# Windowed attention followed by a maxout feed-forward layer: the order of work between chunk 1 and chunk 5 rewritten, and V of chunk 2 requested later

## The chip, the cores and the metric

The kernel runs on one core of a Trainium2 chip. The metric is the device time of one execution in microseconds (us). Work on the core is done by TensorE (PE for matmuls, PEld for the loading of the stationary operand), VectorE (DVE), ScalarE (ACT) and GpSimd (POOL). SyncE (SP) issues most DMAs. Each engine takes its instructions in the order in which the program lists them.

## The reference, cut to what matters

Inputs are q, k and v of 4 batches, 8 heads, 768 positions and 64 dimensions, three weights of 512 x 768 and an output weight of 768 x 512. Each query sees the 4 first positions ("sinks") and the last 128.

```python
scores = scale * np.matmul(q, k.transpose(0, 1, 3, 2))
keep = is_sink | in_window            # rel = i - j; 0 <= rel < 128
scores = np.where(keep, scores, -1e9)
a = softmax(scores)                   # over the keys
x = concat_heads(np.matmul(a, v))     # 3072 x 512
h = np.maximum(np.maximum(x @ w1, x @ w2), x @ w3)
out = h @ w_out                       # 3072 x 512, float32
```

## The kernel before, in words

The 3072 tokens are cut into 12 chunks (`ci`) of 256, three to a batch. A chunk passes through these helpers, each of which emits its instructions on the spot:

- `load` requests q, k or v of a chunk on SP's queue, 512 KB each. Each kind has two buffers, so chunk 3's q goes where chunk 1's was. A `gate` is a one-element write by POOL into the buffer ahead of the load: the load has to wait for it, and so it sets when the load may be issued. `after(wi, c)` copies an element of weight `wi`, column `c`, so POOL first waits until that piece of the weight has landed; `pool_gate` is a plain memset.
- `load_w` and `load_wo` request weights on POOL's own DMA queue: three pieces of 256 columns for each of the three weights (`w1`, `w2`, `w3` of the reference are `w_sb[0]`, `[1]`, `[2]`), two for the output weight.
- `cast_qk` and `cast_v` turn the loaded float32 into bf16 on the engine named in the call; `turn` transposes q or k on PE and copies the result out of PSUM; `turn_dma` does it by a DMA on SP (chunk 4 on).
- `score` (PE), `expo` (ACT) and `mask` (DVE) make the masked exponentials of a pair of heads (`p` = 0 to 3). `sink_score` and `av_open` add the sinks; `av` multiplies with V on PE into a PSUM bank, and then divides by the row sum on DVE (a reciprocal, L476, and a multiplication, L479).
- `xpose` transposes x on PE and copies it out; `xpose_dma` does it by DMA (chunk 3 on).
- `ffn_h(ci, fp, wi)` multiplies a third (`fp`) of the hidden columns with weight `wi`, 8 matmuls, and takes the result from PSUM: for `wi` 0 a copy (ACT as a rule), for 1 and 2 a running maximum on DVE (L527). `ffn_y(ci, t)` is the output product of half a chunk, 6 matmuls.

There are eight PSUM banks. `bank` gives out the one that came free longest ago, in the order of the program, and the matmul that writes it waits for its last reader.

What is run when is an order written out by hand: the calls for chunks 0 to 5 stand one after another (L626 to L877), and a loop with a fixed pattern follows for the chunks after that. While chunk 0 and 1 are still in attention, the weights arrive; the feed-forward work of chunks 0 and 1 is held back and put between the attention work of chunks 1 and 2.

Of the kernel before, what the change touches and what calls it, by code (L numbers as in the profile page):

```python
# [16 lines left out]
def kernel(  # L17
# [13 lines left out]
    nc = tc.nc  # L31
# [12 lines left out]
    DS = d_model // 128  # L44
# [4 lines left out]
    with tc.manual_schedule():  # L49
# [239 lines left out]
        def load_w(wi, c0=0, c1=None):  # L289
            c1 = d_ff if c1 is None else c1  # L290
            w = (moe_w1, moe_w2, moe_w3)[wi]
            nc.gpsimd.dma_start(out=w_sb[wi][:, :, c0:c1],  # L292
                                in_=w.rearrange("(a p) f -> p a f", p=128)[:, :, c0:c1])
# [98 lines left out]
        def expo(ci, p):  # L392
            if ci >= NEW:
                return expo4(ci, p)
            lo = 0 if ci % CPB else 1
            e, st = es[ci, p]
            for a in range(2):
                nc.scalar.activation(e[:, a, lo:], st[a][:, lo:], AF.Exp, scale=scale)  # L398
                give(st[a])
# [43 lines left out]
        os_ = {}  # L443
# [13 lines left out]

        xs = {}

        def av(ci, p):  # L460
            b, c = divmod(ci, CPB)
            o = os_[ci, p]
            e = es[ci, p][0]
            first = c == 0
            for t in range(2):
                for a in range(2):
                    blocks = [(1, ci, 0)] if t == 0 else [(2, ci, 0), (3, ci, 1)]
                    if t == 0 and c:
                        blocks = [(0, ci - 1, 1)] + blocks
                    for s, cv, n in blocks:  # L470
                        nc.tensor.matmul(  # L471
                            o[:, t, a], lhsT=e[:, a, s], rhs=vb[cv % RING][:, n, 2 * p + a],
                            start=first, stop=True, skip_group_check=True)
                        first = False
            rc = work.tile([128, 2, 2], F32, tag="rc", bufs=4, name="rc")
            nc.vector.reciprocal(rc, o[:, :, :, D])  # L476
            if ci not in xs:
                xs[ci] = work.tile([128, NP, 2, 2, D], BF16, tag="x", bufs=2, name="x_sb")
            nc.vector.tensor_mul(xs[ci][:, p], o[:, :, :, 0:D],  # L479
                                 rc.unsqueeze(3).to_broadcast([128, 2, 2, D]))  # L480
            give(o)

        xTs = {}

        def xpose(ci, t, eng=None):
            eng = eng or nc.scalar
            if t == 0:
                xTs[ci] = work.tile([128, DS, 2, 128], BF16, tag="xT", bufs=3, name="xT")
            pt = bank([128, DS, 128], BF16, "xt")
            for ds in range(DS):  # L490
                nc.tensor.transpose(
                    pt[:, ds], xs[ci][:, ds, t].rearrange("q a d -> q (a d)"), ident)
            (nc.scalar.copy if eng is nc.scalar else eng.tensor_copy)(xTs[ci][:, :, t], pt)
            give(pt)
# [6 lines left out]

        hs = {}

        def ffn_h(ci, fp, wi, cuts=1, eng=nc.scalar):
            if ci not in hs:
                hs[ci] = work.tile([128, FB, 256], BF16, tag="h", bufs=3, name="h_sb")
            hp = bank([128, 2, 256], F32, "h_ps")
            for f in range(2):
                c0 = (2 * fp + f) * 128
                for ds in range(DS):  # L510
                    x = xTs[ci][:, ds]
                    if ci < NEW:
# [4 lines left out]
                    nc.tensor.matmul(  # L517
                        hp[:, f].rearrange("q (i t r) -> q i t r", i=2, r=x.shape[3]),
                        lhsT=w_sb[wi][:, ds, c0:c0 + 128], rhs=x,
                        start=(ds == 0), stop=(ds == DS - 1))  # L520
            dst = hs[ci][:, 2 * fp:2 * fp + 2]
            if wi == 0:
                (nc.scalar.copy if eng is nc.scalar else eng.tensor_copy)(dst, hp)  # L523
            else:
                for f in range(cuts):
                    x = slice(2 * f // cuts, 2 * (f + 1) // cuts)
                    nc.vector.tensor_max(dst[:, x], dst[:, x], hp[:, x])  # L527
            give(hp)
# [170 lines left out]
        sink_v(0)  # L699
        expo(1, 3)  # L700
        ffn_h(0, 2, 0, 1, nc.vector)
        score(1, (2,))
        load(2, 'q', part=1, parts=2)
        load(2, 'q', part=0, parts=2, gate=pool_gate)
        load_w(2, 0, 256)
        expo(1, 2)
        load_w(2, 256, 512)
        load_w(2, 512, 768)
        mask(1, 3)
        ffn_h(0, 1, 0)  # L710
        mask(1, 2)
        av_open(1)
        ffn_h(0, 0, 0)
        av(1, 0)
        load(2, 'v', gate=after(0, 300))
        av(1, 3)
        av(1, 1)
        av(1, 2)
        ffn_h(0, 2, 1)
        ffn_h(0, 1, 1)  # L720
        xpose(1, 0, nc.vector)
        xpose(1, 1, nc.scalar)
        ffn_h(0, 0, 1)
        cast_qk(2, 'k', 1, nc.gpsimd)
        ffn_h(1, 2, 0)
        cast_qk(2, 'k', 0, nc.scalar)
        ffn_h(1, 0, 0)
        ffn_h(1, 1, 0)
        load_wo()
        load(3, 'q', gate=after(2, 300))  # L730
        load(3, 'k')
        factors(msk0[0], addm0)
        turn(2, 'k', 0, nc.vector)
        ffn_h(1, 0, 1)
        cast_v(2, 1, 0, nc.gpsimd)
        turn(2, 'k', 1, nc.scalar)
        ffn_h(1, 1, 1)
        cast_qk(2, 'q', 1, nc.scalar)
        cast_qk(2, 'q', 0, nc.vector)
        ffn_h(1, 2, 1)  # L740
        ffn_h(1, 1, 2)
        turn(2, 'q', 1, nc.scalar)
        ffn_h(0, 0, 2)
        turn(2, 'q', 0, nc.scalar)
        ffn_h(0, 1, 2)
        score(2, (0,))
        expo(2, 0)
        score(2, (3,))
        score(2, (1,))
        cast_v(2, 1, 1, nc.gpsimd)  # L750
        sink_score(2)
        expo(2, 1)
        mask(2, 0)
        load(3, 'v', gate=after(1))
        cast_v(2, 0, 0, nc.gpsimd)
        expo(2, 3)
        ffn_h(1, 0, 2)
        cast_v(2, 0, 1, nc.gpsimd)
        ffn_h(0, 2, 2)
        ffn_h(1, 2, 2)  # L760
        score(2, (2,))
        load(4, 'q', gate=after(0, 300))
        cast_qk(3, 'q', 0, nc.gpsimd)
        av_open(2)
        load(4, 'k', gate=after(0))
        mask(2, 1)
        expo(2, 2)
        cast_qk(3, 'k', 0, nc.gpsimd)
        load(4, 'v')
        mask(2, 3)  # L770
        mask(2, 2)
        cast_qk(3, 'q', 1, nc.vector)
        ffn_y(0, 0)
        ffn_y(0, 1)
        av(2, 0)
        turn(3, 'q', 0, nc.scalar)
        cast_qk(3, 'k', 1, nc.scalar)
        load(5, 'q')
        av(2, 2)
        load(5, 'k', gate=after(0, 300))  # L780
        av(2, 3)
        turn(3, 'q', 1, nc.scalar)
        av(2, 1)
        ffn_y(1, 0)
        turn(3, 'k', 1, nc.scalar)
        turn(3, 'k', 0, nc.scalar)
        xpose(2, 0, nc.scalar)
        xpose(2, 1, nc.vector)
        ffn_y(1, 1)
        cast_qk(4, 'q', 1, nc.vector)  # L790
        cast_v(3, 0, 0, nc.gpsimd)
        cast_v(3, 0, 1, nc.gpsimd)
        score(3, (1,))
        cast_v(3, 1, 1, nc.gpsimd)
        cast_qk(4, 'q', 0, nc.vector)
        expo(3, 1)
        score(3, (0,))
        cast_qk(4, 'k', 0, nc.vector)
        cast_qk(4, 'k', 1, nc.gpsimd)
        mask(3, 1)  # L800
        ffn_h(2, 0, 0)
        cast_v(4, 1, 0, nc.gpsimd)
        cast_v(3, 1, 0, nc.vector)
        score(3, (3,))
        turn_dma(4, 'k')
        turn_dma(4, 'q')
        expo(3, 0)
        expo(3, 3)
# [172 lines left out]
```

## Time and profile before

| | us |
|---|---|
| median of 3 runs (lowest to highest) | 176.03 (175.41 to 176.61) |
| the profiled execution, whole | 175.3 |
| its span in the profile | 173.6 |
| TensorE busy | 167.1 |
| VectorE / GpSimd / ScalarE busy | 124.7 / 110.9 / 88.7 |

The profile is of one execution; the difference of 1.7 us between its time and its span lies around the program. The granted TensorE clock was full (1.0) throughout. The 16 DMA engines were at nine tenths or more in nearly every slice of the first 48 us, since inputs and weights come in at the same time there. Times in the profile's views count from the span's start; L numbers are lines of the kernel before.

### The profile page before, as it was taken

The numbers are of one execution on the slowest core, as the hardware profiler recorded it, in microseconds if no ns is written. First come the engines' busy times: TensorE is split into PE (matmuls) and PEld (weight loads), VectorE is DVE, ScalarE is ACT, GpSimd is POOL, SyncE is SP. The second block draws the span as 40 slices with busy tenths as digits, with TensorE's granted clock in tenths as the row PEclk, the third lists the DMA queues.
The fourth block names the chain that finished last, engine by engine and source line by source line (L and its number), as shares of the span: only waits on it lengthen the run. The fifth ranks groups of instructions, "written<-read, shape, count | busy, mean of one in ns | idle before, by whom it ended". The sixth has DMA issues, their size and how long they took to land.

```text
span 173.6 us, 5416 instructions
## 1 busy us (share of the span) xinstructions
PE 167.1 (96%) x2225; PEld 128.6 (74%) x2225; DVE 124.7 (72%) x262; ACT 88.7 (51%) x183; POOL 110.9 (64%) x193
## 2 busy tenths in 40 slices
PE   7979999999999999999999999999999999999992
PEld 2546888857696697797797797797797896896871
DVE  3387854796797985986877976877777776776361
ACT  4778544677954614817726717717636516510210
POOL 7399507545499999999999999999998600000000
PEclk9999999999999999999999999999999999999999
DMA  4999999999999997988999999989999119017303
GB/s 139 301 288 198 218 217 256 221 306 276 280 195 216 190 273 124 245 199 216 253 199 252 195 224 246 265 168 227 264 195 259 32 33 377 21 34 272 121 2 121
DMA packets 71545, 35.22 MB, mean 203 GB/s; under 512 B 27488, under 2 KB 69984, under 8 KB 71520
## 3 DMA queue, kind: packets, MB, share of 16 engines
q1 hardware_dynamic: 65824, 31.60, 79.0%
q0 software_dynamic: 5552, 3.15, 12.7%
q8 instruction: 17, 0.28, 0.7%
q10 hardware_dynamic: 144, 0.13, 0.2%
q14 instruction: 8, 0.07, 0.1%
HBM read 25.17 MB, written 6.29 MB: 181 GB/s over the span
## 4 chain that ended last, share of the span: by engine, by line
PE 85%; DMA 7%; POOL 5%; issue 1%; DVE 0%; POOLq 0%; SPq 0%
PE h_ps L517 52%; PE y_ps L564 11%; PE y_ps L540 7%; PE o L471 6%; DMA w<-in_moe_w_dram 4%; PE st L357 3%; DMA v_raw<-in_v_dram 3%; PE st L331 2%; POOL w L292 2%; POOL vb L123 1%; PE pt L138 1%; PE o L453 1%; PE y_ps L586 1%; PE sk L423 1%; POOL q_bf L118 0%
## 5 line engine op out<-in xcount | busy, mean ns | idle before, releaser
L517 PE MATMUL h_ps<-xT,w 128*128 128x256 bf16 x864 | 101.2, 273 | 0.2 <-DMA w<-in_moe_w_dram 0.2
L517 PEld LDWEIGHTS <-w 128*128 128x128 bf16 x864 | 81.7, 98 | 10.7 <-issue 0.5
L527 DVE TENSOR_TENSOR h_sb<-h_sb,h_ps 128x512 bf16<-128x512 bf16 (+1 forms) x74 | 49.0, 670 | 17.4 <-PE h_ps L517 15.6
L523 ACT CAST h_sb<-h_ps 128x512 bf16<-128x512 f32 x35 | 20.6, 589 | 51.3 <-PE h_ps L517 51.2
L129 POOL CAST vb<-v_raw 32x512 bf16<-32x512 f32 x48 | 36.8, 766 | 2.5 <-DMA v_raw<-in_v_dram 0.3
L90 POOL CAST k_bf<-k_raw 32x512 bf16<-32x512 f32 x48 | 29.6, 616 | 2.2
L398 ACT ACTIVATE e_sb<-st 128x512 bf16<-128x512 f32 (+1 forms) x48 | 23.1, 583 | 1.1 <-PE st L331 1.1
L479 DVE TENSOR_TENSOR x_sb<-o,rc 128x256 bf16<-128x256 f32 x48 | 20.4, 424 | 1.7
L564 PE MATMUL y_ps<-wo,h_sb 64*64 64x512 bf16 (+1 forms) x312 | 21.1, 377 | 0.0
L471 PE MATMUL o<-vb,e_sb 128*128 128x65 bf16 x352 | 16.5, 193 | 0.8 <-DVE vb L123 0.8
L471 PEld LDWEIGHTS <-e_sb 128*128 128x128 bf16 x352 | 14.5, 97 | 3.1 <-ACT e_sb L398 1.0
L123 POOL CAST vb<-v_raw 64x512 bf16<-64x512 f32 x18 | 12.6, 697 | 5.7 <-DMA v_raw<-in_v_dram 5.1
L389 DVE TENSOR_TENSOR e_sb<-e_part,msk 128x1024 bf16<-128x1024 bf16 x16 | 13.1, 831 | 3.3 <-ACT e_part L374 3.1
L406 DVE TENSOR_TENSOR e_sb<-e_sb,msk 128x1024 bf16<-128x1024 bf16 (+1 forms) x18 | 13.6, 776 | 2.3 <-ACT e_sb L398 2.1
L564 PEld LDWEIGHTS <-h_sb 64*64 64x64 bf16 (+1 forms) x312 | 9.9, 106 | 5.0
L374 ACT ACTIVATE e_part<-st 128x384 bf16<-128x384 f32 x32 | 13.1, 495 | 0.5 <-PE st L357 0.5
L540 PE MATMUL y_ps<-wo,h_sb 128*128 128x512 bf16 x54 | 12.8, 380 | 0.0
L476 DVE RECIPROCAL rc<-o 128x4 f32<-128x4 f32 x48 | 8.4, 174 | 4.0 <-PE o L471 3.8
L118 POOL CAST k_bf<-k_raw 128x512 bf16<-128x512 f32 x6 | 3.8, 650 | 9.5 <-PE pt L138 6.8
L118 ACT CAST q_bf<-q_raw 128x512 bf16<-128x512 f32 x13 | 7.6, 620 | 3.0 <-DMA q_raw<-in_q_dram 3.0
L540 PEld LDWEIGHTS <-h_sb 128*128 128x128 bf16 x54 | 4.8, 98 | 5.4 <-DVE h_sb L527 0.8
L427 ACT ACTIVATE e_sink<-sk 128x256 bf16<-128x256 f32 x8 | 3.1, 389 | 10.0 <-PE sk L423 10.0
(90 smaller groups left out, 142.9 us busy)
## 6 DMA issues: line engine op xcount, KB each, us to landing
k_raw<-in_k_dram SPq DMA_DIRECT2D x11, 512.0 KB, 5.6
v_raw<-in_v_dram SPq DMA_DIRECT2D x11, 512.0 KB, 5.6
q_raw<-in_q_dram SPq DMA_DIRECT2D x10, 512.0 KB, 6.9
out_dram<-y_sb SPq DMA_DIRECT2D x9, 512.0 KB, 3.1
w<-in_moe_w_dram POOLq DMA_DIRECT2D x9, 256.0 KB, 6.1
q_raw<-in_q_dram SPq DMA_DIRECT2D x4, 256.0 KB, 7.6
out_dram<-y_sb SPq DMA_DIRECT2D x1, 1024.0 KB, 5.3
wo<-in_moe_w_out_dram POOLq DMA_DIRECT2D x2, 384.0 KB, 8.0
```

The costliest lines, as they stand in the source:

```text
L90: f(bfs[ci, "k"][x:x + 32, :, n], raws[ci, "k"][y:y + 32, :, i].rearrange("q (p a) d -> q p a d", a=2))
L123: eng.tensor_copy(vb[ci % RING][64 * i:64 * i + 64, n, :, 0:D], raws[ci, "v"][64 * n:64 * n + 64, :, i])
L129: eng.tensor_copy(vb[ci % RING][x:x + 32, n, :, 0:D], raws[ci, "v"][y:y + 32, :, i])
L398: nc.scalar.activation(e[:, a, lo:], st[a][:, lo:], AF.Exp, scale=scale)
L406: (eng or nc.vector).tensor_mul(e[:, :, lo:], e[:, :, lo:], msk0[0] if lo else msk)
L471: nc.tensor.matmul(o[:, t, a], lhsT=e[:, a, s], rhs=vb[cv % RING][:, n, 2 * p + a], start=first, stop=True, skip_group_check=True)
L479: nc.vector.tensor_mul(xs[ci][:, p], o[:, :, :, 0:D], rc.unsqueeze(3).to_broadcast([128, 2, 2, D]))
L517: nc.tensor.matmul(hp[:, f].rearrange("q (i t r) -> q i t r", i=2, r=x.shape[3]), lhsT=w_sb[wi][:, ds, c0:c0 + 128], rhs=x, start=(ds == 0 ...
L523: (nc.scalar.copy if eng is nc.scalar else eng.tensor_copy)(dst, hp)
L527: nc.vector.tensor_max(dst[:, x], dst[:, x], hp[:, x])
L540: nc.tensor.matmul(yp, lhsT=hs[ci][:, fb, t * 128:(t + 1) * 128], rhs=wo[:, fb], start=(fb == 0), stop=(fb == FB - 1))
L564: nc.tensor.matmul(yps[ci][t][c:c + cols], lhsT=hs[ci][hp, fb, x:x + cols], rhs=wo[hp, fb], start=(turn == 0 and fb == 0), stop=(turn == 1 ...
```

## The change

The calls from the last scores of chunk 1 to the first casts of chunk 5 stand in another order. So that they can be put more finely, four helpers get a switch: `av(..., then=False)` leaves the division to a later call of `norm`, `ffn_h(..., then=False)` leaves the maximum to a later `ffn_max`, and `xpose` takes the order in which the four pairs are transposed.

```diff
-        def av(ci, p):
+        def av(ci, p, then=True):
...
+            if then:
+                norm(ci, p)
+
+        def norm(ci, p):
+            o = os_[ci, p]
             rc = work.tile([128, 2, 2], F32, tag="rc", bufs=4, name="rc")
             nc.vector.reciprocal(rc, o[:, :, :, D])
...
-        def xpose(ci, t, eng=None):
+        def xpose(ci, t, eng=None, order=range(DS)):
...
-            for ds in range(DS):
+            for ds in order:
...
+            maxima[ci, fp, wi] = hp
+            if then:
+                ffn_max(ci, fp, wi, cuts, eng)
+
+        def ffn_max(ci, fp, wi, cuts=1, eng=nc.scalar):
+            hp = maxima.pop((ci, fp, wi))
...
-        load(2, 'v', gate=after(0, 300))
...
+        load(2, 'v', gate=after(2, 600))
...
-        cast_v(2, 1, 1, nc.gpsimd)
...
+        cast_v(2, 1, 1, nc.vector)
...
-        cast_v(2, 0, 1, nc.gpsimd)
...
+        cast_v(2, 0, 1, nc.vector)
```

No instruction is added or taken away, and each stays on its engine, but for the two casts of V of chunk 2 that go from POOL to DVE.

The last scores of chunk 1 (pair 2) now come after `av_open(1)` and `av(1, 1)`; `ffn_h(0, 1, 1)` comes after the transposes of chunk 1 rather than ahead of them; `ffn_h(1, 2, 0)` and `(1, 1, 0)` come ahead of `ffn_h(0, 0, 1)`, the first user of the last piece of weight 1. Three `ffn_y` halves come ahead of `av_open(2)` where there were two. The transposes of chunk 3 come ahead of `ffn_y(1, 1)` and those of x of chunk 2 after it; three scores of chunk 3 come ahead of `ffn_h(2, 0, 0)` rather than two.

The first place is on VectorE, at chunk 1: `e_sb` is what `mask` works on, `rc` and `x_sb` are the division after `av`, `h_sb` a maximum or copy of the feed-forward. Before:

```order
L523 CAST h_sb<-h_ps 128x512
L406 TENSOR_TENSOR e_sb<-e_sb,msk 128x1024 x2
L476 RECIPROCAL rc<-o 128x4
L479 TENSOR_TENSOR x_sb<-o,rc 128x256
L476 RECIPROCAL rc<-o 128x4
L479 TENSOR_TENSOR x_sb<-o,rc 128x256
```

After, with the numbers of the new lines:

```order
L536 CAST h_sb<-h_ps 128x512
L406 TENSOR_TENSOR e_sb<-e_sb,msk 128x1024
L481 RECIPROCAL rc<-o 128x4
L484 TENSOR_TENSOR x_sb<-o,rc 128x256
L406 TENSOR_TENSOR e_sb<-e_sb,msk 128x1024
L481 RECIPROCAL rc<-o 128x4
L484 TENSOR_TENSOR x_sb<-o,rc 128x256
```

The first division (pair 1, which needs no mask) moves between the two masks; three divisions follow as before.

The second place is on GpSimd, where gates, weight requests and casts share one queue: `w_109` is weight 2, `w_107` weight 0, `v_raw` and `q_raw` the buffers that a gate writes to, `vb_79` V of chunk 2 in bf16. Before:

```order
L602 CAST k_raw<-w_107 1x1
L606 MEMSET q_raw 1x1
L292 DMA w_109<-in_moe_w_dram 128x4x256 x3
L602 CAST v_raw<-w_107 1x1
L118 CAST k_bf<-k_raw 128x2x2x2x64
L300 DMA wo<-in_moe_w_out_dram 128x3x512 x2
L602 CAST q_raw<-w_109 1x1
L238 TENSOR_SCALAR msk_0_101<-addm_99 128x384 x2
L123 CAST vb_79<-v_raw 64x8x64 x2
L602 CAST v_raw<-w_108 1x1
L123 CAST vb_79<-v_raw 64x8x64 x2
```

After:

```order
L615 CAST k_raw<-w_107 1x1
L292 DMA w_109<-in_moe_w_dram 128x4x256
L619 MEMSET q_raw 1x1
L292 DMA w_109<-in_moe_w_dram 128x4x256 x2
L118 CAST k_bf<-k_raw 128x2x2x2x64
L300 DMA wo<-in_moe_w_out_dram 128x3x512 x2
L238 TENSOR_SCALAR msk_0_101<-addm_99 128x384 x2
L615 CAST v_raw<-w_109 1x1
L615 CAST q_raw<-w_109 1x1
L615 CAST v_raw<-w_108 1x1
L615 CAST q_raw<-w_107 1x1
L123 CAST vb_79<-v_raw 64x8x64
```

The gate of V of chunk 2 moves behind the output weight's requests and reads weight 2 instead of weight 0. The gates of q of chunk 3, v of chunk 3 and q of chunk 4 now follow it directly. On SP's queue the load of V of chunk 2 keeps its place, after q of chunk 2 and ahead of q of chunk 3.

The third place is on VectorE, ahead of the first `av` of chunk 2. Before:

```order
L406 TENSOR_TENSOR e_sb<-e_sb,msk 128x1024
L527 TENSOR_TENSOR h_sb<-h_sb,h_ps 128x512 x3
L406 TENSOR_TENSOR e_sb<-e_sb,msk 128x1024 x3
L118 CAST q_bf<-q_raw 128x2x2x2x64
L476 RECIPROCAL rc<-o 128x4
```

After:

```order
L540 TENSOR_TENSOR h_sb<-h_sb,h_ps 128x512 x4
L406 TENSOR_TENSOR e_sb<-e_sb,msk 128x1024 x3
L123 CAST vb_79<-v_raw 64x8x64
L540 TENSOR_TENSOR h_sb<-h_sb,h_ps 128x512
L118 CAST q_bf<-q_raw 128x2x2x2x64
L406 TENSOR_TENSOR e_sb<-e_sb,msk 128x1024
L123 CAST vb_79<-v_raw 64x8x64
L481 RECIPROCAL rc<-o 128x4
```

The two casts of V now stand between the masks and the divisions, with the cast of q of chunk 3 between them; `av(2, 0)` needs the second of them.

Of the DMAs that SP issues later, `turn_dma(4, 'q')` now comes ahead of `turn_dma(4, 'k')`, `load(6, 'q')` ahead of `xpose_dma(3)`, and `load(5, 'v')` behind it.

More of the change, by code (lines that the diff above doesn't have):

```diff
@@ L755 @@
+        sink_score(2)
+        ffn_h(0, 2, 2)
+        mask(2, 1)
+        expo(2, 0)
+        mask(2, 0)
+        load(4, 'q', gate=after(0, 300))
+        expo(2, 3)
+        cast_v(2, 1, 0, nc.gpsimd)
+        mask(2, 3)
+        score(2, (2,))
+        load(4, 'k', gate=after(0))
         cast_v(2, 0, 0, nc.gpsimd)
-        expo(2, 3)
-        ffn_h(1, 0, 2)
-        cast_v(2, 0, 1, nc.gpsimd)
-        ffn_h(0, 2, 2)
+        load(4, 'v')
+        cast_v(2, 1, 1, nc.vector)
         ffn_h(1, 2, 2)
-        score(2, (2,))
@@ L762 @@
[L762 to L766, printed above, removed]
-        expo(2, 2)
[L768 to L772, printed above, removed]
+        expo(2, 2)
         ffn_y(0, 0)
         ffn_y(0, 1)
+        cast_qk(3, 'q', 0, nc.gpsimd)
+        ffn_y(1, 0)
+        av_open(2)
+        cast_qk(3, 'q', 1, nc.vector)
+        cast_qk(3, 'k', 0, nc.gpsimd)
@@ L833 @@
+        ffn_h(2, 2, 1)
         sink_k(1)
```

142 lines of the change are left out of this document (73 added, 69 removed).

## The prediction

> **What bounds the kernel now.** I read the page first: its busy times, and which engines the chain that ended last runs through.
>
> ```profile
> span 173.6 us, 5416 instructions
> PE 167.1 (96%) x2225; PEld 128.6 (74%) x2225; DVE 124.7 (72%) x262; ACT 88.7 (51%) x183; POOL 110.9 (64%) x193
> PE 85%; DMA 7%; POOL 5%; issue 1%; DVE 0%; POOLq 0%; SPq 0%
> ```
>
> TensorE has the chain nearly to itself. The change lies between the first `ffn_h` (15.86) and the end of the last `ffn_h` of chunk 2 (54.08), so I asked for the busy time of each engine in two stages, up to the end of TensorE's one wait there and from it on (the first column behind the stage is its length).
>
> ```profile
> core 0: us, PE busy (x) PEld busy (x) DVE busy (x) ACT busy (x) POOL busy (x), PEclk, DMA share, GB/s
> 15.86:22.73 6.87, 6.71 (x94) 5.44 (x95) 5.28 (x14) 4.05 (x10) 3.97 (x9) 1.00 1.40 212
> 22.73:54.08 31.35, 31.35 (x349) 24.50 (x350) 22.92 (x49) 19.58 (x39) 17.49 (x33) 1.00 1.18 251
> ```
>
> TensorE is idle for 0.16 us in the first stage and not at all in the second. A busy PE need not be PE at its peak, so I price the work at its pitch in the chain of waits, where overlap is taken out (start, duration, what; the last row is TensorE's timeline at its wait).
>
> ```profile
> 16.59 6.10 DMA w<-in_moe_w_dram
> ...
> 31.50 0.22 PE pt L138 x4
> 31.73 0.87 PE h_ps L517 x8
> 32.60 0.77 PE st L331 x18
> ...
> 36.32 0.33 PE st L331 x6
> 36.65 0.23 PE o L453 x8
> ...
> 40.74 0.24 PE o L471 x8
> 40.98 1.29 PE y_ps L540 x6
> ...
> 44.47 0.44 PE st L331 x8
> ...
> 22.73 3.67 PE L517 MATMUL h_ps<-xT,w 128*128 128x256 bf16 x32 [0.17 <-DMA w<-in_moe_w_dram]
> ```
>
> The stretch holds 27 `ffn_h` (23.5), four `ffn_y` halves (5.2), scores of chunks 1 to 3 (0.33 + 1.10 + 0.88), sinks (3 x 0.23), `av` of three chunks (8 x 0.24, and 4 x 0.18 for the 6 matmuls of a pair in chunk 3), and 12 transposes of four (12 x 0.22): 36.9 us. It takes 54.08 - 15.86 = 38.2. So 1.3 us is all that any order of these instructions can gain: the wait of 0.17 at 22.73 with its refill (32 matmuls took 3.67 there, and four times 0.87 is 3.48), and some ten seams of about 0.1. That is 0.7% of the time; nothing behind the stretch is removed.
>
> **Chunk 1, 15.9 to 22.7.** What TensorE could wait for are ACT's exponentials and DVE's masks and divisions.
>
> ```profile
> 16.34 0.41 ACT L427 ACTIVATE e_sink<-sk 128x256 bf16<-128x256 f32 x1
> 16.61 2.11 ACT L398 ACTIVATE e_sb<-st 128x512 bf16<-128x512 f32 x4
> ...
> 17.84 0.69 DVE L406 TENSOR_TENSOR e_sb<-e_sb,msk 128x1024 bf16<-128x1024 bf16 x1 [0.22 <-ACT e_sb L398]
> ...
> 19.68 0.18 DVE L476 RECIPROCAL rc<-o 128x4 f32<-128x4 f32 x1 [0.24 <-PE o L471]
> ...
> 20.24 0.17 DVE L476 RECIPROCAL rc<-o 128x4 f32<-128x4 f32 x1
> ...
> 21.95 0.61 PE L491 MATMUL xt<-ident,x_sb 128*128 128x128 bf16 x8
> ```
>
> `av_open(1)` now follows `ffn_h(0, 2, 0)` and needs the sinks' exponential, done at 16.75: PE gets there at 16.73, so no more than 0.1 is lost. `av(1, 1)` (0.24) and the scores (0.33) bring PE to 17.6; the next bank is free once pair 3's exponentials are read, 16.61 + 1.05 = 17.7. `ffn_h(0, 1, 0)` ends at 18.55, the mask that `av(1, 3)` needs at 18.53. On DVE a division takes 0.56 (19.68 to 20.24). Mask, division, mask, three divisions from 17.84 end at about 21.4. PE, with two `av`, `ffn_h(0, 0, 0)`, one `av` and `ffn_h(0, 2, 1)`, is at 21.07, does three transposes by 21.2 and waits 0.2 for the fourth pair; the new order of pairs puts that one last. The transposes end at 21.7, and `ffn_h(0, 1, 1)`, now behind them, at 22.65. Before, the same work ended at 22.56 and PE waited until 22.73, with 0.19 of refill. The piece of weight 1 for which it waited lands at 16.59 + 6.10 = 22.69 and is first used two `ffn_h` later: the wait goes, and nothing is late in its place, since the copies of x have the 0.87 of `ffn_h(0, 1, 1)` as cover. Gain 0.2 to 0.3.
>
> **V of chunk 2.** Its load is issued 10 us later than before. These are the landing times of the transfers in question, by windows of the DMA view that hold one issue each of POOL (weight 2's last piece) and SP, then V of chunk 2, q of chunk 3 and V of chunk 5 (KB, us from issue to landing); below them the issue times, and the cast that waited for k of chunk 3.
>
> ```profile
> w<-in_moe_w_dram POOLq DMA_DIRECT2D x1, 256.0 KB, 11.4
> q_raw<-in_q_dram SPq DMA_DIRECT2D x1, 256.0 KB, 11.4
> ...
> v_raw<-in_v_dram SPq DMA_DIRECT2D x1, 512.0 KB, 11.6
> ...
> q_raw<-in_q_dram SPq DMA_DIRECT2D x1, 512.0 KB, 8.8
> ...
> v_raw<-in_v_dram SPq DMA_DIRECT2D x1, 512.0 KB, 4.1
> ...
> 17.53 2.23 POOL L292 DMA_DIRECT2D w<-in_moe_w_dram  x3
> ...
> 20.54 2.05 SPq L107 DMA_DIRECT2D v_raw<-in_v_dram  x1
> ...
> 29.00 0.37 SPq L107 DMA_DIRECT2D q_raw<-in_q_dram  x1
> ...
> 51.14 0.53 SPq L107 DMA_DIRECT2D v_raw<-in_v_dram  x1
> ...
> 40.44 0.62 POOL L118 CAST k_bf<-k_raw 128x512 bf16<-128x512 f32 x1 [1.13 <-DMA k_raw<-in_k_dram]
> ```
>
> Weight 2's last piece (issued at 17.53 + 2 x 0.74) landed at 30.4, q of chunk 2 (issued about 18.9) at 30.3, V at 32.1, then q of chunk 3 at 37.8 and its k at 40.4. SP's transfers land in their order, so V was already moved after weight 2; requested early, it only stood in line. That is why I expect no gain from this edit: it frees no bandwidth before 30.3. What it can cost is a gap: POOL's gate passes at 30.4, SP issues at about 30.6, with nothing in line. Queued behind the gate on POOL are the gates of q and v of chunk 3 and q of chunk 4, and on SP the loads of chunk 3. V then lands at 30.6 + 4.1 = 34.7 at best (as V of chunk 5, with little beside it) and 30.6 + 8.8 = 39.4 at worst; q of chunk 3 between 36.5 (1.8 later, as V came after q before) and 40.4 (5.7 later, as q came after V beside the output weight). I take 35.5 and 38, since before the two and the output weight together were in by 37.8.
>
> The Trainium skill, "DMA: Bandwidth & Descriptors" (Queues, rings and completion order), has each DMA engine go round robin between the queues that have work; by that rule the gap would be filled by the output weight and q of chunk 3 would still land at 37.8, with no cost. No row here shows one queue alone in this stretch, so I keep the gap in the range.
>
> **Who waits for it.** PE from 22.65: 12 `ffn_h`, four transposes, scores and sinks end `ffn_h(0, 2, 2)` at 22.65 + 10.5 + 0.88 + 0.77 + 0.22 = 35.0; another score, another `ffn_h`, three `ffn_y` and `av_open` bring it to `av(2, 0)` at 40.4 with one seam. DVE from 35.1 (the last row is the V casts' shortest, median and longest in ns):
>
> ```profile
> 36.36 0.69 DVE L527 TENSOR_TENSOR h_sb<-h_sb,h_ps 128x512 bf16<-128x512 bf16 x1 [0.19 <-PE h_ps L517]
> 36.96 2.30 DVE L406 TENSOR_TENSOR e_sb<-e_sb,msk 128x1024 bf16<-128x1024 bf16 x3
> 39.19 0.41 DVE L118 CAST q_bf<-q_raw 128x512 bf16<-128x512 f32 x1
> ...
> L123 DVE CAST vb<-v_raw x6: 421/424/747, 8.5 to 46.9; 64x512 bf16<-64x512 f32 x6
> ```
>
> Maximum 0.69, three masks 2.30, V 0.42, maximum 0.69, q 0.41, mask 0.77, V 0.42 make 5.7, so 40.8, or 40.5 with the overlap of about 0.07 that neighbours show. `av(2, 0)` loses 0.1 to 0.4; I take 0.2. The cast of q stands at about 39.0, a microsecond behind my 38. The price of V on DVE is its 0.42 on this path; POOL is spared two casts.
>
> The Trainium skill, "SBUF — State Buffer" (Who interferes with whom), says that GpSimd and VectorE in a two-port mode, which its copies and casts can enter, take an exclusive lock on one port pair, so that the loser waits for a whole instruction. The casts' spread above, 421 to 747 ns, agrees that some are held up; by the rule it speaks against casting V on VectorE beside a busy GpSimd.
>
> The maximum of `ffn_h(1, 2, 2)` comes at 39.2, `ffn_y(1, 0)` reads it in its fifth matmul at 39.7: hidden, by 0.5. K of chunk 3 is turned by PE at 42.0 (40.4 and four `av` of 0.24 and two transposes of 0.22 later, with the 0.2); before, it was cast on POOL by 41.1.
>
> **The rest.** These rows are SP's transfer of x of chunk 3, POOL's casts of V of chunk 5, and ACT's copy of x of chunk 2.
>
> ```profile
> 53.36 1.24 SPq L498 DMA_TRANSPOSE xT<-x_sb  x1
> ...
> 61.30 2.62 POOL L123 CAST vb<-v_raw 64x512 bf16<-64x512 f32 x4
> ...
> 43.75 0.62 ACT L493 COPY xT<-xt 128x512 bf16<-128x512 bf16 x1
> ```
>
> V of chunk 5 is now requested behind the transfer, at 54.6 instead of 51.1; with 4.1 in flight it is there by 58.7, and POOL casts it at 61.3: hidden, by 2.6. X of chunk 2 is now transposed behind `ffn_y(1, 1)`, whose 1.29 used to cover the copy of 0.62; three scores (0.66) cover it now, and ACT first copies out that `ffn_y`. I charge 0.15. Scores that now follow an `av` or a transpose instead of an `ffn_h` take away one or two seams, 0.15. The banks that the split divisions and the held maximum keep longer have their next writer at least one `ffn_h` behind the last reader, by the order: nothing, and at most one DVE operation (0.69) if DVE falls behind.
>
> The sum: -0.25 (chunk 1) - 0.15 (seams) + 0.2 (V) + 0.15 (x) = -0.05. The profiled execution took 175.3, 1.7 above its span, and would take 175.25; the median was 176.03, 0.7 higher, so I forecast 176.0.
>
> **Rivals.** *The gap stays.* Slower: SP's line runs dry at 30.3, and all later loads come late by as much as q of chunk 3. It decides from 39.0 on: each microsecond past that holds DVE's cast of q, behind it the last mask and the last cast of V, and so `av(2, 0)`. At 40.4 that is 1.4, and with K of chunk 3 behind it as before (2.6 later, 43.0, and a cast of 0.62, against 43.4 for a PE that is late already) 1.7: 177.7. At 41.5, which needs the line to stay behind by 3.7 us, it is 2.5 and 178.5. For it: V lands beside the output weight. Against: 1 us of room, and the total of bytes is the same. *The seams close.* Faster: longer runs of `ffn_h` take back most of the 1.3, giving 175.0. For it: runs of seven `ffn_h` in place of four; against: most switches between kinds of work remain. *It doesn't do what it says*: V comes no later in line, and the forecast contains that already. *A held cast*: two V casts at 747 ns rather than 424 move `av(2, 0)` by 0.65 and give 176.6; the median of the six casts is the short one.
>
> **The numbers.** Forecast, within 0.5 of 176.0: 0.57. Gap of 0.5 to 1.7, or held casts: 0.17; gap beyond that: 0.13. Seams: 0.10; a gain above 1.7, for which the stretch has no room and which would need something behind 54: 0.03. One per cent, 1.76 us, is what a measurement of this kernel can tell from no change: faster 0.03, within 0.84, slower 0.13. The range goes from the seams' 175.0 to the gap's 177.7; it leaves out about 0.15.
>
> **What would show it.** Right: no wait of PE for weights at 22.7; V of chunk 2 landing at 34 to 37 and q of chunk 3 by 39; `av(2, 0)` near 40.5; the last `ffn_h` of chunk 2 ending within 0.5 of 54.1. Wrong: idle PE between 40 and 43 put down to DVE or V, DMA slices below nine tenths near 31, or a chunk period behind 60 that differs.

## The result, and the profile after

| | before | changed |
|---|---|---|
| median of 20 runs each (lowest to highest), us | 175.94 (175.40 to 177.38) | 177.23 (176.35 to 178.81) |
| ratio, 95% interval | | 1.0070 (1.0049 to 1.0090) |
| the profiled execution, us | 175.3 | 176.57 |
| its span, us | 173.6 | 174.8 |

The change costs 0.7%. The forecast was 176.0 and no change; 177.23 lies inside its range. L numbers from here on are the changed kernel's: `ffn_h` is L524, its maximum L540, the divisions L481 and L484, the copy of x L498, `ffn_y` L553 and L555, the transfer of x L503. The page of the changed kernel, its busy times and its chain:

```profile
span 174.8 us, 5419 instructions
PE 167.3 (96%) x2225; PEld 128.8 (74%) x2225; DVE 126.3 (72%) x264; ACT 88.8 (51%) x183; POOL 109.6 (63%) x191
PE 83%; DVE 4%; DMA 4%; ACT 3%; SPq 2%; POOL 1%; issue 1%; POOLq 0%
```

TensorE is as busy as before; DVE now has 4% of the chain, ACT 3%. Three stages show where the time went: from the first `ffn_h` to `ffn_y(0, 0)`, from there to the end of chunk 2's last `ffn_h`, and on to `ffn_h(3, 0, 0)`, the first of chunk 3. Before:

```profile
15.86:36.80 20.94, 20.77 (x250) 17.20 (x251) 13.81 (x28) 12.45 (x26) 10.34 (x21) 1.00 1.29 233
36.80:54.15 17.35, 17.35 (x208) 12.80 (x204) 14.45 (x35) 11.19 (x23) 11.18 (x21) 1.00 1.13 258
54.15:58.26 4.11, 4.11 (x48) 1.78 (x49) 3.17 (x6) 3.77 (x9) 3.84 (x11) 1.00 1.02 154
```

After:

```profile
15.93:36.40 20.47, 20.47 (x243) 17.38 (x244) 13.17 (x27) 11.92 (x25) 7.49 (x17) 1.00 1.26 220
36.40:54.83 18.43, 17.89 (x210) 12.96 (x211) 16.10 (x38) 11.75 (x25) 12.36 (x22) 1.00 1.07 246
54.83:59.54 4.71, 4.19 (x49) 1.86 (x49) 3.99 (x8) 4.34 (x9) 4.37 (x12) 1.00 1.17 200
```

The first stage before also holds `av_open(2)` (0.23), which now comes in the second. So the first became 0.24 shorter, the second 0.85 longer, the third 0.60 longer: 1.21, which is the whole difference of the spans. Inside the second stage, TensorE's timeline and DVE's say who was late:

```profile
40.61 0.20 PE L471 MATMUL o<-vb,e_sb 128*128 128x65 bf16 x1
41.24 0.87 PE L471 MATMUL o<-vb,e_sb 128*128 128x65 bf16 x23 [0.43 <-DVE vb L123]
...
35.29 0.69 DVE L540 TENSOR_TENSOR h_sb<-h_sb,h_ps 128x512 bf16<-128x512 bf16 x1 [1.28 <-PE h_ps L524]
35.89 2.30 DVE L406 TENSOR_TENSOR e_sb<-e_sb,msk 128x1024 bf16<-128x1024 bf16 x3
38.23 0.84 DVE L123 CAST vb<-v_raw 64x512 bf16<-64x512 f32 x1
39.10 0.69 DVE L540 TENSOR_TENSOR h_sb<-h_sb,h_ps 128x512 bf16<-128x512 bf16 x1
39.71 0.42 DVE L118 CAST q_bf<-q_raw 128x512 bf16<-128x512 f32 x1
40.04 0.69 DVE L406 TENSOR_TENSOR e_sb<-e_sb,msk 128x1024 bf16<-128x1024 bf16 x1
40.76 0.42 DVE L123 CAST vb<-v_raw 64x512 bf16<-64x512 f32 x1
```

DVE ran without a pause from 35.29 until the last cast of V was done at 41.18. In the traces without the wait the 24 matmuls take 0.90 together; here they end at 42.11 and not at 41.51, so `av(2, 0)` lost 0.60. Two of DVE's operations were longer than usual: the third mask (1.10 from 37.10, the first two 0.69 each) and the first cast of V (0.84, where the last cast of V took 0.42). Each began while GpSimd was casting V itself:

```profile
37.01 0.64 POOL L123 CAST vb<-v_raw 64x512 bf16<-64x512 f32 x1 [4.86 <-DMA v_raw<-in_v_dram]
38.18 0.60 POOL L123 CAST vb<-v_raw 64x512 bf16<-64x512 f32 x1
```

TensorE was idle for 18.43 - 17.89 = 0.54 in the second stage, 0.43 of it at `av(2, 0)` and 0.11 ahead of `ffn_h(2, 0, 0)`, where the chain below has ACT's copy of x. So of the other 0.25, 0.14 is left that no wait accounts for. The third stage is in the chain of waits:

```profile
44.58 0.59 ACT y_sb L555
45.16 0.50 ACT xT L498
45.66 0.04 issue
45.70 1.91 PE h_ps L524 x16
...
55.98 3.54 ACT e_sb L398 x7
59.52 0.02 issue
59.54 1.92 PE h_ps L524 x16
```

`ffn_h(3, 0, 0)` waited 0.52, and the chain names ACT's exponentials, done at 59.52. X of chunk 3, which SP transposes, was no earlier: issued at 54.37 and 5.1 in flight, it landed at 59.47. `a_vload`, a run below with the same order of calls but for one load, shows which of the two counted. Its chain and ACT's timeline:

```profile
53.69 4.78 DMA xT<-x_sb
58.47 0.05 issue
58.52 1.92 PE h_ps L524 x16
...
54.90 4.03 ACT L398 ACTIVATE e_sb<-st 128x512 bf16<-128x512 f32 x8
```

There `ffn_h(3, 0, 0)` started 0.05 behind the landing of x, while the exponentials ran on to 58.93: it waits for x, and in the changed kernel's chain the exponentials only happened to end 0.05 behind the landing. Before, x was issued at 53.36, took 4.8 and landed at 58.16, just ahead of the `ffn_h` at 58.26, so that transfer had no slack to start with. Counted from the start of the third stage it landed at 4.01 before and at 4.64 after: it was issued 0.33 later against TensorE's own work, and was 0.3 longer in flight.

Last, the DMA view from 27 to 35 us (40 slices of 0.2 us, GB/s), before and after:

```profile
GB/s 215 218 212 207 218 223 225 212 238 284 305 333 325 340 340 338 335 305 241 233 220 230 225 213 210 205 210 200 197 210 207 233 202 218 220 215 207 230 230 261
```

```profile
GB/s 210 210 223 212 218 207 220 215 243 249 174 126 90 28 46 113 223 200 215 200 220 200 220 179 200 195 205 200 205 200 205 210 210 282 297 320 330 330 340 335
```

Where the first had V of chunk 2 in line and moved 300 GB/s and more, the second falls to 28: nothing stood in SP's line until POOL's gate let V go at 31.01. V landed 5.9 us later, at 36.9, q of chunk 3 at 31.48 + 7.1 = 38.6.

### The profile page after: what moved, and what is told of

It is laid out like the page before. It is cut to its first block, busy times and chain, and to the rows that moved or that the text cites. A ratio compares the mean times of both kernels' runs of the same rounds, so it can differ in the third digit from the quotient of the medians.

```text
span 174.8 us, 5419 instructions
## 1 busy us (share of the span) xinstructions
PE 167.3 (96%) x2225; PEld 128.8 (74%) x2225; DVE 126.3 (72%) x264; ACT 88.8 (51%) x183; POOL 109.6 (63%) x191
## 4 chain that ended last, share of the span: by engine, by line
PE 83%; DVE 4%; DMA 4%; ACT 3%; SPq 2%; POOL 1%; issue 1%; POOLq 0%
PE h_ps L524 54%; PE y_ps L577 11%; PE o L471 6%; DMA v_raw<-in_v_dram 4%; PE st L357 3%; PE y_ps L553 3%; ACT e_sb L398 2%; SPq L107 2%; DVE e_sb L406 2%; PE st L331 2%; DVE vb L123 1%; PE pt L138 1%; PE o L453 1%; PE sk L423 1%; DVE h_sb L540 1%
## 5 line engine op out<-in xcount | busy, mean ns | idle before, releaser
L524 PE MATMUL h_ps<-xT,w 128*128 128x256 bf16 x864 | 101.0, 273 | 0.7 <-ACT e_sb L398 0.5
L524 PEld LDWEIGHTS <-w 128*128 128x128 bf16 x864 | 81.9, 98 | 11.1 <-DMA xT<-x_sb 1.0
L540 DVE TENSOR_TENSOR h_sb<-h_sb,h_ps 128x512 bf16<-128x512 bf16 (+1 forms) x74 | 49.3, 671 | 21.9 <-PE h_ps L524 19.8
L484 DVE TENSOR_TENSOR x_sb<-o,rc 128x256 bf16<-128x256 f32 x48 | 20.4, 424 | 1.7
L123 POOL CAST vb<-v_raw 64x512 bf16<-64x512 f32 x16 | 11.3, 704 | 7.8 <-DMA v_raw<-in_v_dram 7.2
L389 DVE TENSOR_TENSOR e_sb<-e_part,msk 128x1024 bf16<-128x1024 bf16 x16 | 13.8, 886 | 3.0 <-ACT e_part L374 3.0
L406 DVE TENSOR_TENSOR e_sb<-e_sb,msk 128x1024 bf16<-128x1024 bf16 (+1 forms) x18 | 12.8, 728 | 2.1 <-ACT e_sb L398 2.1
L553 PE MATMUL y_ps<-wo,h_sb 128*128 128x512 bf16 x54 | 12.7, 380 | 0.0
L481 DVE RECIPROCAL rc<-o 128x4 f32<-128x4 f32 x48 | 8.4, 175 | 3.8 <-PE o L471 3.6
L553 PEld LDWEIGHTS <-h_sb 128*128 128x128 bf16 x54 | 5.0, 98 | 5.6 <-DVE h_sb L540 1.0
```

What stands on the lines that cost most here:

```text
L389: nc.vector.tensor_mul(x.rearrange("q a (t s) c -> q (a t) s c", t=2), y, msk2)
L406: (eng or nc.vector).tensor_mul(e[:, :, lo:], e[:, :, lo:], msk0[0] if lo else msk)
L484: nc.vector.tensor_mul(xs[ci][:, p], o[:, :, :, 0:D], rc.unsqueeze(3).to_broadcast([128, 2, 2, D]))
L524: nc.tensor.matmul(hp[:, f].rearrange("q (i t r) -> q i t r", i=2, r=x.shape[3]), lhsT=w_sb[wi][:, ds, c0:c0 + 128], rhs=x, start=(ds == 0 ...
L553: nc.tensor.matmul(yp, lhsT=hs[ci][:, fb, t * 128:(t + 1) * 128], rhs=wo[:, fb], start=(fb == 0), stop=(fb == FB - 1))
```

## The experiments

All were timed in five rounds beside the kernel before; each line gives the ratio to it with its 95% interval. Unless said, the edit is against the changed kernel.

**Parts of the change undone.** `a_vload` requests V early again; `a_vcast` leaves it late and puts the two casts on GpSimd, where they stand; `a_xpose` restores x ahead of `ffn_y(1, 1)`; `a_vx` is the first and third together.

```diff
 load_w(2, 512, 768)
+load(2, 'v', gate=after(0, 300))     # a_vload, a_vx
...
-load(2, 'v', gate=after(2, 600))     # a_vload, a_vx
...
-cast_v(2, 1, 1, nc.vector)           # a_vcast
+cast_v(2, 1, 1, nc.gpsimd)
...
-cast_v(2, 0, 1, nc.vector)           # a_vcast
+cast_v(2, 0, 1, nc.gpsimd)
...
-ffn_y(1, 1)                          # a_xpose, a_vx
 xpose(2, 0, nc.scalar)
 xpose(2, 1, nc.vector)
+ffn_y(1, 1)
```

> The changed kernel with V of chunk 2 requested where it was before (behind weight 2's requests, gated on weight 0). Late V (its casts reach POOL at 37.0 and run beside VectorE's, whose first cast of V took 0.84 instead of 0.42): V lands near 32, the cast on VectorE takes 0.42, TensorE's wait at av(2, 0) shrinks from 0.6 to 0.2 or less, and the ratio goes from 1.007 to about 1.004. X behind y (the transposes of x of chunk 2 behind ffn_y(1, 1) make VectorE and ACT late): no more than the wait at 41 goes, and the waits at 45.7 and 59.5 stay, since VectorE still starts its casts at 45. Line (SP's order of transfers behind 46 makes x of chunk 3 late): 1.006 or more.

> The changed kernel with all four casts of V of chunk 2 on POOL, the load as late as changed. If VectorE's two casts are what costs at av(2, 0), the wait shrinks by 0.4 or more: 1.004. If the late landing (37.0) is the cause, POOL has four casts of 0.62 in line from 37.0 with gates and q of chunk 3 between them, the last ends near 41 to 42, and av(2, 0) waits as long or longer: 1.007 to 1.012.

> The changed kernel with ffn_y(1, 1) behind the two transposes of x of chunk 2, as before. X behind y: ffn_h(2, 0, 0) no longer waits for ACT's copy (0.25 to 0.3 back), VectorE copies x 1.3 earlier and does its casts for chunk 4 in the gap, the last division of chunk 3 comes about 0.7 earlier, x of chunk 3 lands earlier and the wait of 0.5 at 59.5 shrinks or goes: 0.5 to 0.8 us back, ratio about 1.003. Late V: only the 0.3 at 45.7 comes back, 1.0055. Line: the wait at 59.5 stays at 0.5 although the division is earlier.

> Both of these edits together. Late V and x behind y as two separate causes: the gains add up to 1.0 to 1.3 us, ratio 0.999 to 1.002. If one of the two feeds the other (VectorE late from 38 on), the gain of both is less than the sum: 1.003. Line: 1.004 or more.

Measured: `a_vload` 1.0075 (1.0048 to 1.0102), `a_vcast` 1.0070 (1.0044 to 1.0096), `a_xpose` 1.0135 (1.0103 to 1.0168), `a_vx` 1.0056 (1.0035 to 1.0077). No part given back alone gave the time back, and the gains that "Late V" and "X behind y" expected did not come. The trace of `a_vload` does show what late V did to DVE. With V early, GpSimd's casts of V were over at 34.11 and nothing was held up: three masks took 1.89 and not 2.30, the cast 0.43 and not 0.84, and DVE was through at 40.37, ahead of `av(2, 0)`, which did not wait:

```profile
35.92 1.89 DVE L406 TENSOR_TENSOR e_sb<-e_sb,msk 128x1024 bf16<-128x1024 bf16 x3
37.84 0.43 DVE L123 CAST vb<-v_raw 64x512 bf16<-64x512 f32 x1
...
39.95 0.42 DVE L123 CAST vb<-v_raw 64x512 bf16<-64x512 f32 x1
```

But this profiled execution was the fastest of its six (175.54, median 177.01), so why the others were slow has to come from the runs that follow. In `a_vcast`, TensorE's timeline at `av(2, 0)`, the wait only changed hands, since its last cast stands behind GpSimd's casts of q and k of chunk 3; in `a_xpose`, x was transposed sooner and then waited for DVE's division:

```profile
41.85 0.86 PE L471 MATMUL o<-vb,e_sb 128*128 128x65 bf16 x23 [1.19 <-POOL vb L123]
```

```profile
42.28 0.87 PE L471 MATMUL o<-vb,e_sb 128*128 128x65 bf16 x23 [0.78 <-DVE vb L123]
...
45.04 0.56 PE L496 MATMUL xt<-ident,x_sb 128*128 128x128 bf16 x7 [0.70 <-DVE x_sb L484]
```

So `ffn_y(1, 1)` ahead of x is not what costs here: it covers late divisions.

**The order by thirds.** The new order was cut at the first scores of chunk 2 and behind the transposes of its x. Each of `h_head`, `h_mid` and `h_tail` is the kernel before with one third new and V requested early; `h_headmid` is the changed kernel with its last third as before.

> The kernel before with only the first third of the new order, from the last scores of chunk 1 up to the first scores of chunk 2 (V of chunk 2 requested early as before). Middle (the loss comes from what stands ahead of VectorE's divisions of chunk 2: casts of V and of q): this third is not the cause, it saves the wait of 0.17 and its refill at 22.7, ratio 0.998 to 1.001. Head (the loss comes from what the new first third does to the transfers: q of chunk 3 and the output weight later): 1.004 or more.

> The kernel before with only the second third of the new order, from the first scores of chunk 2 to the transposes of x of chunk 2 (V early). Middle: TensorE waits at av(2, 0) and the division of chunk 2 ends about 0.6 later against TensorE's work, ratio 1.004 to 1.008. Head or tail: 1.000 to 1.002.

> The kernel before with only the last third of the new order, from the casts of chunk 4 and the scores of chunk 3 to the end of the change. Middle: 0.999 to 1.002. Tail (the loss comes from VectorE's new order there, with k of chunk 4 and V of chunk 3 cast between the masks of chunk 3, so that x of chunk 3 is transferred late and ffn_h(3, 0, 0) waits): ratio 1.004 or more, and the wait of 0.5 at about 58.5 stands in the trace.

> The changed kernel with the last third of the order as before (V late). Middle: as the changed kernel, 1.005 to 1.008. Tail: 1.003 or less. Head: as the changed kernel.

Measured: 0.9989 (0.9967 to 1.0011), 1.0100 (1.0064 to 1.0136), 1.0000 (0.9974 to 1.0025), 1.0061 (1.0033 to 1.0089). The middle third carries the loss, and alone it cost more than expected. DVE in `h_headmid` (V late) shows how:

```profile
38.61 0.69 DVE L540 TENSOR_TENSOR h_sb<-h_sb,h_ps 128x512 bf16<-128x512 bf16 x1
40.17 0.43 DVE L118 CAST q_bf<-q_raw 128x512 bf16<-128x512 f32 x1 [0.87 <-DMA q_raw<-in_q_dram]
40.51 1.10 DVE L406 TENSOR_TENSOR e_sb<-e_sb,msk 128x1024 bf16<-128x1024 bf16 x1
41.64 0.42 DVE L123 CAST vb<-v_raw 64x512 bf16<-64x512 f32 x1
```

The cast of q of chunk 3 waits for its DMA; the mask and the last cast of V, whose data is long there, stand behind it. The mask is held up besides (1.10), by GpSimd's cast of q, which starts on the same landing (40.29).

**Off the line behind q.** All with V requested early. `e_order` moves the q cast behind the divisions, `f_order2` only behind the last V cast; `f_one` moves the last V cast to GpSimd, `e_pool` both; `e_pool_y` is `e_pool` with before's places of the two `ffn_y`; `b_xlate` is the kernel before with `ffn_y(1, 1)` ahead of x.

```diff
-cast_qk(3, 'q', 1, nc.vector)        # e_order, f_order2
...
 mask(2, 2)
 cast_v(2, 0, 1, nc.vector)
+cast_qk(3, 'q', 1, nc.vector)        # f_order2
...
 av(2, 3)
+cast_qk(3, 'q', 1, nc.vector)        # e_order
```

```diff
+cast_v(2, 0, 1, nc.gpsimd)           # f_one, ahead of the third cast; e_pool, behind it
-cast_v(2, 1, 1, nc.vector)           # e_pool
+cast_v(2, 1, 1, nc.gpsimd)           # e_pool
...
-cast_v(2, 0, 1, nc.vector)           # f_one, e_pool
```

> The changed kernel with V of chunk 2 requested early, and VectorE's cast of q of chunk 3 moved from ahead of mask(2,2) to behind the divisions of av(2,3); TensorE's, ScalarE's, GpSimd's and SyncE's orders untouched. 'The q cast' (in most executions q of chunk 3 lands after 39, and mask(2,2), the last V cast and the divisions stand behind its cast on VectorE): most of the loss goes, 0.998 to 1.002 of before, and in the profile the first division starts at 41.1 or earlier. 'V casts on VectorE' (the chain is too long whatever q does): 1.004 to 1.007. 'ScalarE's copy of x' (x behind ffn_y(1,1)): unchanged, 1.005 to 1.0075.

> The changed kernel with V of chunk 2 requested early and all four of its casts on GpSimd, one behind the other and ahead of GpSimd's casts for chunk 3; the q cast stays where the change put it. 'The q cast': av(2,0) no longer waits for a V cast, but mask(2,2) and the divisions still stand behind q: part of the loss stays, 1.003 to 1.006. 'V casts on VectorE': 0.998 to 1.002. 'ScalarE's copy of x': 1.005 to 1.0075.

> As the run with all V casts on GpSimd and, besides, before's places of ffn_y: ffn_y(1,0) behind av(2,1) instead of ahead of av(2,0), ffn_y(1,1) behind the transposes of x of chunk 2. av(2,0) stands at 39 to 39.5 on TensorE then. 'The q cast': 1.004 to 1.010, since the mask behind q is needed 1.3 us sooner. 'V casts on VectorE': 1.000 to 1.003. 'ScalarE's copy of x': 0.998 to 1.002, lower than the run without this part.

> The kernel before with one edit: ffn_y(1,1) ahead of the two transposes of x of chunk 2, as the change has it. 'ScalarE's copy of x': TensorE waits 0.3 us for the copy before ffn_h(2,0,0), and the time is 1.002 to 1.006. 'The q cast' and 'V casts on VectorE': 0.999 to 1.002, the copy is on the path but the divisions are not waited for any more.

Measured: `e_order` 1.0055 (1.0030 to 1.0081), `e_pool` 1.0006 (0.9980 to 1.0031), `e_pool_y` 0.9985 (0.9959 to 1.0011), `b_xlate` 1.0015 (0.9981 to 1.0049). `e_order` settles nothing, because I had put the q cast too far back and PE, turning q, waited for it:

```profile
43.19 0.40 PE L138 MATMUL pt<-ident,q_bf 128*128 128x128 bf16 x4 [1.31 <-DVE q_bf L118]
```

`e_pool` is as fast as before, so the casts on DVE matter; whether by their 0.42 us or by their place was the next question. `b_xlate` shows the predicted wait for ACT's copy in its trace (0.28), too small to tell in the time.

> The changed kernel with V of chunk 2 requested early and one move on VectorE: the cast of q of chunk 3 from ahead of mask(2,2) and the last V cast to right behind them, ahead of the first division. 'V behind q' (the last V cast stands behind a cast that waits for q, which landed anywhere between 38.2 and 40.5 in the traces, and av(2,0) waits for it): 0.998 to 1.003, TensorE starts av(2,0) without a wait. 'A cast on VectorE costs by itself' (its 0.42 us, twice, or their clash with GpSimd's casts): 1.004 to 1.007.

> The changed kernel with V of chunk 2 requested early and only the last V cast taken from VectorE and put on GpSimd ahead of its casts for chunk 3; the third V cast stays on VectorE, and so does the q cast in its place. 'V behind q': as the run with all V casts on GpSimd, 0.999 to 1.003. 'A cast on VectorE costs by itself': half of the loss stays, 1.003 to 1.005.

Measured: `f_order2` 1.0005 (0.9987 to 1.0022), `f_one` 1.0003 (0.9985 to 1.0021). Both keep a V cast or two on DVE and both repair the time; only the place behind q is gone. "A cast on VectorE costs by itself" falls, for V requested early. TensorE and DVE in `f_order2`:

```profile
40.66 0.90 PE L471 MATMUL o<-vb,e_sb 128*128 128x65 bf16 x24
...
37.87 0.43 DVE L123 CAST vb<-v_raw 64x512 bf16<-64x512 f32 x1
38.33 0.69 DVE L540 TENSOR_TENSOR h_sb<-h_sb,h_ps 128x512 bf16<-128x512 bf16 x1
38.94 0.68 DVE L406 TENSOR_TENSOR e_sb<-e_sb,msk 128x1024 bf16<-128x1024 bf16 x1
39.65 0.42 DVE L123 CAST vb<-v_raw 64x512 bf16<-64x512 f32 x1
40.11 0.72 DVE L118 CAST q_bf<-q_raw 128x512 bf16<-128x512 f32 x1
```

Its three stages are 20.49, 17.83 and 4.17: the third is again as before (4.11), and of the second 17.83 - 17.58 = 0.25 is left, which is not the casts'. One thing is argued, not seen: the trace of `a_vload` has no wait at `av(2, 0)` either. That its median is slow through the place behind q rests on the times of `f_order2` and `f_one`, and on `h_mid`, whose trace with early V has the wait (0.18):

```profile
39.72 0.43 DVE L118 CAST q_bf<-q_raw 128x512 bf16<-128x512 f32 x1
40.06 1.10 DVE L406 TENSOR_TENSOR e_sb<-e_sb,msk 128x1024 bf16<-128x1024 bf16 x1
41.19 0.42 DVE L123 CAST vb<-v_raw 64x512 bf16<-64x512 f32 x1
```

The q cast began only 0.07 behind the operation ahead of it; most of the delay is the mask, 1.10 beside GpSimd's cast of q at 39.84. So a last V cast behind q can be late in two ways, by q's landing and by GpSimd's cast of q beside the mask, and the times do not tell their shares.

**Late V by itself.** `f_late_pool` takes the place behind q away but leaves V late: all four casts on GpSimd ahead of those for chunk 3. `b_vlate` is the kernel before with the late request alone.

```diff
 factors(msk0[0], addm0)              # b_vlate
+load(2, 'v', gate=after(2, 600))
...
-load(2, 'v', gate=after(0, 300))
```

> The changed kernel with all four V casts on GpSimd, ahead of its casts for chunk 3, and the request for V of chunk 2 where the change put it, behind weight 2. Four casts of 0.65 to 0.8 us behind a landing at 36.7 to 38.2 end at 39.5 to 41.2, and av(2,0) needs the last at 40.6. 'V behind q' alone: 1.000 to 1.004. 'Late V costs too, once the casts are repaired': 1.004 to 1.008.

> The kernel before with one edit: V of chunk 2 requested behind weight 2 (behind the factors, ahead of q of chunk 3), as the change has it; all casts of V stay on GpSimd in before's places, two of them ahead of its cast of q of chunk 3. 'Late V costs by itself': V lands at 36.5 to 38.2, the four casts end at 39.5 to 41, av(2,0) stands at 39.4 in this order and waits up to 1.5 us, later loads shift: 1.004 to 1.010. 'Late V costs only in the new order': 0.999 to 1.002.

Measured: `f_late_pool` 1.0066 (1.0043 to 1.0090), `b_vlate` 1.0122 (1.0085 to 1.0158). Late V costs by itself, in the old order most of all, and there more than the 1.010 expected. TensorE and GpSimd in `b_vlate`, then TensorE in `f_late_pool`:

```profile
41.94 0.37 PE L471 MATMUL o<-vb,e_sb 128*128 128x65 bf16 x7 [1.48 <-POOL vb L123]
42.73 0.40 PE L138 MATMUL pt<-ident,q_bf 128*128 128x128 bf16 x4 [0.42 <-POOL q_bf L118]
...
37.86 2.15 POOL L123 CAST vb<-v_raw 64x512 bf16<-64x512 f32 x2 [6.49 <-DMA v_raw<-in_v_dram]
40.53 1.36 POOL L123 CAST vb<-v_raw 64x512 bf16<-64x512 f32 x2
```

```profile
59.74 0.94 PE L524 MATMUL h_ps<-xT,w 128*128 128x256 bf16 x7 [0.95 <-DMA xT<-x_sb]
```

In `b_vlate` four casts in a row on GpSimd behind a V that is first cast at 37.86 hold `av(2, 0)`, and the q cast behind them holds the turning of q. In `f_late_pool` the 24 matmuls from `av(2, 0)` on take 1.12, 0.22 more than without a wait, and most of the loss is at x of chunk 3: issued at 54.2, it was 5.5 us in flight, against 4.7 in `f_order2`, and the third stage is 5.18 long. Why it was longer in flight is not shown.

**Faster than both?** `f_best` is `e_pool_y` with mask(2, 2) ahead of the q cast; `h_ht` is `h_head` with the new last third.

> An attempt at a faster kernel than both: the new order with V of chunk 2 requested early, its casts all on GpSimd, ffn_y(1,0) and ffn_y(1,1) in before's places, and mask(2,2) ahead of VectorE's cast of q. 'V behind q': nothing of av(2) stands behind q any more, 0.995 to 0.999 (the wait of 0.25 us in chunk 1 gone, ScalarE's copy hidden again). Other theories: no lower than the same without the mask's move, 0.9985 and more.

> An attempt at a faster kernel than both: the new order up to the first scores of chunk 2 with V of chunk 2 requested early, before's order from there to the transposes of x of chunk 2, and the new order behind the casts for chunk 4. If the middle third alone carries the loss and the head's wait of 0.25 us is a gain: 0.996 to 0.9995. If the gain of the head is taken back by the next wait: 0.9995 to 1.002.

Measured: 1.0010 (0.9988 to 1.0032) and 1.0018 (0.9993 to 1.0043). Neither beats the kernel before, and no run did by more than its interval. For `f_best` "V behind q" had expected a gain, which did not come.

| order | V requested | last V cast | ratio |
|---|---|---|---|
| before | early | GpSimd, ahead of q's | 1 |
| before | late | GpSimd, ahead of q's | 1.0122 |
| new | late | VectorE, behind q's (the change) | 1.0070 |
| new | late | GpSimd, behind q's (`a_vcast`) | 1.0070 |
| new | late | GpSimd, ahead of q's | 1.0066 |
| new | early | VectorE, behind q's | 1.0075 |
| new | early | VectorE, ahead of q's | 1.0005 |
| new | early | GpSimd, ahead of q's | 1.0003, 1.0006 |

The change has two faults. Either costs 0.7% with the other repaired, and both together cost no more. That is why giving back one part at a time showed nothing. Why the two do not add up is not shown: in the traces both make `av(2, 0)` late, but most of what late V costs in `f_late_pool` is at x of chunk 3.

## Why the prediction was wrong

The direction failed: no change was forecast, and the kernel got 0.7% slower. Term by term the forecast was -0.25, -0.15, +0.2 and +0.15; the traces have -0.24, +0.14, +0.60 and +0.11, and +0.60 at a place where the sum has no term.

*Chunk 1, -0.25.* Right: the first stage is 0.24 shorter, one run of 64 matmuls from 21.75 with no wait for weight 1. Whether it reaches the end isn't known: `h_head`, which has it alone, is 0.9989 (0.9967 to 1.0011), which fits the full gain as well as none.

*Seams, -0.15, and x of chunk 2, +0.15.* The chain after shows ACT's copy of `ffn_y(1, 1)` and then of x, 1.09 together, ahead of `ffn_h(2, 0, 0)`, as charged; the wait is 0.11, and 0.28 in `h_mid`, `h_headmid` and `b_xlate`, where two scores and not three cover the copy. No gain of seams appeared: with the casts repaired, `f_order2` still has the second stage 0.25 longer, 0.14 without that wait. The 0.15 that I credited isn't there, and what the 0.14 consists of is open.

*V of chunk 2.* "V then lands at 30.6 + 4.1 = 34.7 at best ... I take 35.5 and 38". It landed at 36.9, and q at 38.6, inside the bounds. The gap itself was foreseen ("with nothing in line"). What failed is to price it by the landing of V and q alone: the early request kept the DMAs fed at 29 to 30 us, and dropping it costs 1.2% in the old order (`b_vlate`). The prediction drew from the rule of the Trainium skill, "DMA: Bandwidth & Descriptors" (Queues, rings and completion order), that the output weight would fill the gap; it did not: the slices fall to 28 GB/s although that weight was requested from 27.31 on. Between 30.5 and 31.3 POOL's queue moved 206 GB/s by itself; why it moved so little just before is not shown.

*Who waits for it, +0.2.* "`av(2, 0)` loses 0.1 to 0.4; I take 0.2." This is the mis-sized term: 0.60. The wait was named rightly, DVE's line ahead of the last V cast: 5.89 from 35.29 to 41.18, against 5.7, or 5.4 with the overlap. What failed is the price of its operations, taken from the kernel before as if it were fixed. The first V cast took 0.84 where I took 0.42, and TensorE lost 0.17 more than the 0.43 that it was idle. The three masks did take the 2.30 that I took, but by luck: in the kernel before, the third of them was held beside GpSimd's cast of q (37.98), and in the changed kernel beside its cast of V. Without these two holds, as in `a_vload`, the line is 5.05 and there is no wait. So late V costs here by bringing GpSimd's casts of V beside DVE's line, and not by a wait for V or q. Besides, the q cast in the line waits for a DMA that lands differently from run to run.

*The rest.* "V of chunk 5 ... hidden" was right, but the same sentence's transfer, x of chunk 3 on SP, was put at nothing without a reason. It ends where `ffn_h(3, 0, 0)` starts, with 0.1 to spare before, so being issued 0.33 later against TensorE and flying 0.3 longer is charged there nearly in full: +0.60. The sum by stages is -0.24 + 0.60 + 0.25 + 0.60 = 1.21, and I had -0.05.

*The rivals.* The 1.2 us by which the kernel is slower than forecast lie in the case "gap of 0.5 to 1.7, or held casts", to which I gave 0.17. "The gap stays" came nearest in time: its 177.7 is 0.5 from the median of 177.23. Its first step is in the trace (the line ran dry), and its route, q, mask, last V cast, `av(2, 0)`, is what `f_order2` and `f_one` repair with V early. But that its price is near is in part luck: in the profiled execution q landed at 38.6, below the 39.0 from which it decides, no cast of q waited, and half of the loss stands at x of chunk 3, which that price doesn't hold. "A held cast" happened once (0.84), and a mask was held too: that is the loss at `av(2, 0)`. "It doesn't do what it says" fell: V landed 4.8 us later than before. "The seams close" fell.

*The signs.* V (36.9) and q (38.6) landed where a right forecast wanted them, and no weight was waited for at 22.7; the last `ffn_h` of chunk 2 ended 0.7 late. The idle TensorE put down to DVE's V cast at 41 and the thin DMA slices near 30 were the signs of being wrong. Behind the third stage both kernels take 115.3 us, so nothing later differs.

## What to carry to other kernels

A load that "only stands in line" still keeps the line full: before delaying one, look in the DMA view for what moves at that moment instead. On an engine that takes its work in order, a cast that waits for a DMA belongs behind the work others wait for, but ahead of its own reader; both sides were missed in these runs (the change itself and `e_order`). When giving back parts of a change one at a time shows nothing, there may be two faults whose costs do not add up: cut the change by place, then repair in pairs. A price read from a row holds for what ran beside it: ask which other engine was busy then.

## What the runs showed of the hardware that was not expected

The same operation on DVE had two durations, depending on GpSimd. A cast of 64x512 took 0.84 us at 38.23 in the changed kernel, with GpSimd casting V at 38.18, and 0.43 in `f_order2` at 37.87, with GpSimd idle; the mask of 128x1024 took 1.10 beside a GpSimd cast in `h_headmid` and 0.68 without. This fits the Trainium skill, "SBUF — State Buffer" (Who interferes with whom), where the loser waits for the port.

Landing times spread from run to run although the requests stand at the same place: V requested early was first cast at 32.58 in one trace (`e_order`), 34.65 in another (`e_pool`) and 35.95 in a third (`a_vx`). With such a spread, an order that needs a landing at a given microsecond has to be judged by medians; the changed kernel's own runs reach from 176.35 to 178.81.
